# An adaLN decode step: the last 96 rows of the gate's modulation regrouped, from five pieces to four, and dealt over other transfers

## The chip, the cores and the metric

The kernel runs on one core of one Trainium2 chip. The metric is the device time of one execution in microseconds (us); less is better. Times are medians of several runs. One more execution was taken with the hardware profiler; all rows quoted as profile come from it. Engines: PE (TensorE), DVE (VectorE), ACT (ScalarE), POOL (GpSimd), SP (SyncE, which here only issues transfers), and 16 DMA engines that move the data.

## The reference

One decode step of a transformer block with modulation from a condition `c`, for a batch of 2 and one token each:

```
mod = silu(c) @ w_mod                 # 512 -> 6 * 512: sa, ca, ga, sb, cb, gb
h = layernorm(x) * (1 + ca) + sa
x = x + ga * attention(h)             # 32 heads of 128, 4096 cached positions each
h = layernorm(x) * (1 + cb) + sb
x = x + gb * (mish(h @ w1 + b1) @ w2) # 512 -> 1376 -> 512
```

`gb`, the last gate, is the sixth block of `mod`: `silu(c)` (512 values for each of the two) times `w_mod[:, 2560:3072]`, a matrix of 512 x 512. The change is about how a part of that matrix comes into the core. Nearly all bytes are the caches of keys and values.

## The kernel before

All inputs are laid out on the host as a sequence of loads. Each load fills a tile `room` of 128 partitions with up to 64 KB in each; three such tiles take turns, and a load is issued when the tile's earlier contents have been used. `load(n)` issues the transfers of load `n` on SP's queue: whole transfers of 128 rows at L153, and for a transfer with fewer rows (a "loose" one), four transfers that take every fourth row, at L156 (`STEP = 4`).

A head's keys are multiplied with the query on DVE (`products`, L336) and summed (`sums`, L339). The softmax's weights go to PE, where `weighted_v` (L379) multiplies them with the head's values. After the last head come, in this order on PE: the last head's values, the output projection (`head_out_q`), the norm, the modulation of the second half, the first dense layer (`w1ps`, L573), the transposes back (`fps`, L588), the hidden layer's activation on DVE and ACT (L602 to L609), and the second dense layer (`yps`, L618), eleven groups of four products. `busy(n)` (L316) issues products of `n` blocks of 128 columns whose result nobody reads, two blocks a product; they keep PE going between steps. A float32 product shows in the profile as two matmuls (x2).

The gate's matrix has 512 rows. They are multiplied in `modulation_5` (L538), one term after another into one sum in PSUM:

- `M5 = 3` blocks of 128 rows, which come with the last load;
- `REST` = 32 rows that lie in an otherwise empty part of the second layer's first chunk;
- the other 96 rows, in "pieces". Each piece is a row group on the first partitions of a tile, 512 columns (2 KB) a row. `PIECES = (20, 20, 20, 20, 16)`: the first four stand side by side in one array `m5p` of 20 rows of 8 KB, the fifth in an array `m5q` of 16 rows of 2 KB.

The last two loads look like this (a part is a list of contents and the widths of its transfers, in float32 numbers a row):

```
[([("m5q", 0)], (512,)), ([("m4", 0)] + last[6:], (W + HALF, W, W)), ([("m5p", 0)], (512 * WHOLE,))],
[
    ([("m3", 0), ("w1", 0)], (W + 2 * sum(WIDTHS), 2 * sum(WIDTHS))),
    ([("m5", 0), ("w2", 0)], (512 * (M5 + 1), 5 * 512, 3 * 512, 512, 512)),
],
```

So the last load but one has four transfers of 4 rows of 2 KB (`m5q`), three transfers with the fifth modulation block and the last head's values (3072, 1024 and 1024 KB), and four transfers of 5 rows of 8 KB (`m5p`). The last load has seven transfers of 128 rows, 2400 KB down to 256 KB. On PE, terms 0 and 1 are multiplied before the norm, 2 and 3 during it, term 4 (`m5q`) between `h2ps` and `w1ps`, and the rest after `fps`.

Of the kernel before, what the change touches and what calls it, by code (L numbers as in the profile page):

```python
# [8 lines left out]
F32 = mybir.dt.float32  # L9
# [4 lines left out]
P = 128  # L14
WIDTHS = (384, 384, 352, 256)
CHUNKS = [(g, j) for j in range(3) for g in range(4) if WIDTHS[g] > P * j]
STEP = 4
PIECES = (20, 20, 20, 20, 16)
WHOLE = PIECES.count(PIECES[0])
M5 = 3  # L20
REST0 = WIDTHS[2] - 2 * P
REST = 512 - P * M5 - sum(PIECES)
# [3 lines left out]
W = 2048  # L26
HALF = BIG // 2
SIZES = {
    "k": BIG, "v": HALF, "wq": W, "wo": W, "m01": 2 * W, "m2": W, "m3": W, "m4": W, "m5": 512 * M5,
    "m5p": 512 * WHOLE, "m5q": 512, "w1": 4 * sum(WIDTHS), "w2": 512 * len(CHUNKS),  # L30
}
OUT_STEP = 1
AHEAD = (14, 22)
# [3 lines left out]
def stream():  # L37


    order, n_v = [], 0  # L40
    for h in range(1, HEADS):
        order.append(("k", h))
        if h % HC == HC - 1 and HC < h < HEADS - 1:
            c = (h + 1) // HC
            order.append([("wq", c), ("wo", c - 2)])
        if h not in AHEAD:
            order += [("v", n_v, 0), ("v", n_v, 1)]
            n_v += 1
    order = [x if isinstance(x, list) else [x] for x in order]

    def size(x):
        return sum(SIZES[key[0]] for key in x)

    loads = [[([("m01", 0), ("wq", 0), ("wq", 1)], (4 * W,)), ([("k", 0)], (BIG,))]]
    for _ in range(1, HEADS):
        row = []
        while size(row) < ROW:
            room = ROW - size(row)
            row += order.pop(next(i for i, x in enumerate(order) if size(x) <= room))
        loads.append([(row, (ROW,))])  # L60
    last = [("v", h, i) for h in range(HEADS - 4, HEADS) for i in range(2)]
    assert order == [[key] for key in last[:2]], order
    loads += [
        [(last[:2] + [("wo", 6), ("wo", 7), ("m2", 0)], (BIG + 3 * W,))],
        [(last[2:4], (BIG,)), (last[4:6], (BIG,))],
        [([("m5q", 0)], (512,)), ([("m4", 0)] + last[6:], (W + HALF, W, W)), ([("m5p", 0)], (512 * WHOLE,))],
        [
            ([("m3", 0), ("w1", 0)], (W + 2 * sum(WIDTHS), 2 * sum(WIDTHS))),
            ([("m5", 0), ("w2", 0)], (512 * (M5 + 1), 5 * 512, 3 * 512, 512, 512)),
        ],  # L70
    ]
    return loads
# [3 lines left out]
def kernel(  # L76
# [17 lines left out]
    nc = tc.nc  # L94
# [4 lines left out]
    G = D // P  # L99
# [8 lines left out]
    NCH = len(CHUNKS)  # L108
    NP5 = len(PIECES) + 1

    const = ctx.enter_context(tc.tile_pool(name="const", bufs=1))
# [13 lines left out]
    def take(t, keys):  # L125
        lo = 0
        for key in keys:
            kind, n = key[:2]
            part = t[:, lo : lo + SIZES[kind]]
            lo += SIZES[kind]  # L130
            if kind == "k":
                k_t[n] = part.rearrange("p (j d) -> p j d", d=DH)
            elif kind == "v":
                v_t[n, key[2]] = part.rearrange("p (c n) -> p c n", n=512)
            elif kind in ("wq", "wo"):
                (wq_t if kind == "wq" else wo_t)[n] = part.rearrange("p (k n) -> p k n", k=G)
            else:
                w_t[kind] = part.rearrange("p (k n) -> p k n", k={"w2": NCH, "m5": M5, "m5p": WHOLE, "m5q": 1}.get(kind, G))

    w_t = {}  # L140
    done = set()

    def load(n):

        t = kvp.tile([P, ROW], F32, tag="room", name=f"room{n}", bufs=3)
        lo = 0
        for keys, srcs in loads[n]:
            take(t[:, lo:], keys)
            for src in srcs:
                rows, width = src.shape  # L150
                dst = t[:rows, lo : lo + width]
                if rows == P:
                    nc.sync.dma_start(out=dst, in_=src)  # L153
                else:
                    for i in range(STEP):
                        nc.sync.dma_start(out=dst[i::STEP], in_=src[i::STEP])  # L156
                lo += width

    loaded = 0

    def used(*keys):
# [26 lines left out]
        out=fold, in_=ident.rearrange("p (g r) -> p r g", g=G), axis=AX.X, op=ALU.add  # L188
# [3 lines left out]
        out=mean_w, in0=fold[:, None, :].to_broadcast([P, G, R]), scalar1=1.0 / D, scalar2=None, op0=ALU.mult  # L192
# [4 lines left out]
        out=half, in_=ident.rearrange("p (b r) -> p r b", b=B), axis=AX.X, op=ALU.add  # L197
# [5 lines left out]
    for b in range(B):  # L203
        nc.vector.memset(same[PB * b : PB * (b + 1), b, :], 1.0)
    same = same.rearrange("p b r -> p (b r)")
    eps_t = const.tile([P, 48], F32, name="eps_t")
    nc.vector.memset(eps_t, EPS)

    ct = const.tile([P, G, R], F32, name="ct")
# [2 lines left out]
    ct5 = const.tile([P, NP5, R], F32, name="ct5")  # L212
# [99 lines left out]
    def busy(n, bank=1):  # L312

        for lo in range(0, n, 2):
            cols = P * min(2, n - lo)
            nc.tensor.matmul(ov[bank][:, :cols], lhsT=ident, rhs=e_t[0].rearrange("p c m -> p (c m)")[:, :cols], start=True, stop=True)  # L316
# [131 lines left out]
    for h in range(H):  # L448
# [38 lines left out]
        out=ct5[:, :, ::TB],  # L487
# [38 lines left out]
    w1_t, w2_t = w_t["w1"], w_t["w2"]  # L526
    gps = ov[1 - N % 2][:, :P]
    rest5 = slice(REST0, REST0 + REST)
    wm5p = [w_t["m5p"][:, n, :] for n in range(WHOLE)] + [w_t["m5q"][:, 0, :]]
    terms5 = [(ct5[:rows, n, :], wm5p[n][:rows]) for n, rows in enumerate(PIECES)]  # L530
    terms5 += [(ct[:, k, :], wm5[:, k, :]) for k in range(M5)]
    terms5.append((ct5[rest5, len(PIECES), :], w2_t[rest5, 0, :]))

    def modulation_5(lo, hi):
        for n in range(lo, hi):
            c, w = terms5[n]
            for g in range(G):
                nc.tensor.matmul(  # L538
                    gps[R * g : R * (g + 1)], lhsT=c, rhs=w[:, P * g : P * (g + 1)],
                    start=(n == 0), stop=(n == len(terms5) - 1),  # L540
                )
# [20 lines left out]
    h2ps = columns(hq, "h2ps")  # L562
    nc.vector.tensor_copy(h2t[:, :, ::TB], h2ps)

    busy(1)
    modulation_5(4, len(PIECES))
    hq_pad = work.tile([P, 512], F32, tag="o", name="hq_pad")
    nc.gpsimd.memset(hq_pad[:, : NJ * P], 0.0)
    w1ps = wide_ps("w1ps")
    for k in range(G):  # L570
        lo = 0
# [9 lines left out]
    lo = 0  # L581
# [49 lines left out]
def _lay_out(np, a):  # L631


    def rows(w):

        return w.reshape(-1, P, w.shape[-1]).transpose(1, 0, 2)

    def q_rows(v):

        return v.reshape(2, 4, P).transpose(1, 0, 2).reshape(8, P)  # L640

    B, H, S, DH = a["A_k_cache"].shape
    kv = {
        kind: a[n].reshape(B, H, P // B, -1).transpose(1, 0, 2, 3).reshape(H, P, -1)
        for kind, n in (("k", "A_k_cache"), ("v", "A_v_cache"))
    }
    wq = rows(a["A_wq"]).reshape(P, 4, 8, 512).transpose(2, 0, 1, 3).reshape(8, P, -1)
    wo = a["A_wo"].reshape(8, 4, P, 512).transpose(0, 2, 1, 3).reshape(8, P, -1)
    wm = rows(a["w_mod"])
    w1 = rows(a["B_w1"])  # L650
    starts = np.cumsum((0,) + WIDTHS)
    b1c = np.zeros((P, 12 + 2 * (len(PIECES) + 1)), a["B_b1"].dtype)
    m5 = a["w_mod"][:, 512 * 5 :]
    m5p, f0 = np.zeros((P, len(PIECES) + 1, 512), m5.dtype), P * M5
    for n, size in enumerate(PIECES + (REST,)):
        to = REST0 if n == len(PIECES) else 0
        b1c[to : to + size, 12 + 2 * n : 14 + 2 * n] = a["c"].reshape(2, 512)[:, f0 : f0 + size].T
        m5p[to : to + size, n] = m5[f0 : f0 + size]
        f0 += size
    w2 = np.zeros((P, len(CHUNKS), 512), a["B_w2"].dtype)  # L660
    for n, (g, j) in enumerate(CHUNKS):
        f0 = starts[g] + P * j
        f1 = min(f0 + P, starts[g + 1])
        b1c[: f1 - f0, n] = a["B_b1"][f0:f1]
        w2[: f1 - f0, (n + 1) % len(CHUNKS)] = a["B_w2"][f0:f1]
    w2[REST0 : REST0 + REST, 0] = m5p[REST0 : REST0 + REST, -1]

    pieces = {**kv, "wq": wq, "wo": wo, "m01": [wm[:, :, :1024]], "w1": [w1], "w2": [w2], "m5p": [m5p[:, :WHOLE]], "m5q": [m5p[:, WHOLE]], "m5": [rows(m5)[:, :M5]]}
    for n in (2, 3, 4):
        pieces[f"m{n}"] = [wm[:, :, 512 * n : 512 * (n + 1)]]  # L670
    def piece(kind, n, part=None):
        row = pieces[kind][n].reshape(P, -1)
        return row if part is None else row[:, HALF * part : HALF * (part + 1)]

    loose = {"m5p": PIECES[0], "m5q": PIECES[-1]}
    arrays = {
        "head": np.stack([q_rows(a["c"]), q_rows(a["A_x"])], axis=1),
        "b1c": b1c,
    }
    for n, parts in enumerate(stream()):  # L680
        for i, (keys, widths) in enumerate(parts):
            row = np.concatenate([piece(*key) for key in keys], axis=1)
            cuts = np.split(row, np.cumsum(widths)[:-1], axis=1)
            for j, t in enumerate(cuts):
                arrays[f"load{n}_{i}_{j}"] = np.ascontiguousarray(t[: loose[keys[0][0]]] if keys[0][0] in loose else t)
    return arrays
# [28 lines left out]
```

## Time and profile before

| what | us |
|---|---|
| median of 3 runs (lowest to highest) | 695.18 (695.08 to 695.32) |
| profiled execution, whole time | 694.79 |
| its span, first to last instruction | 693.4 |
| DVE busy | 588.4 (85%) |
| PE busy, matmuls | 291.3 (42%) |
| last head's last values have landed | 672.9 from the span's start |
| the output's transfer is issued | 691.8 from the span's start |

The difference between span and whole time lies around the program's instructions. In rows of the chain, the numbers are the start and the length in us, then the engine, the tile written, and the line. In rows of the timeline stand start, length, engine, line, operation, tiles, shapes, count, and in brackets how long the engine was idle before and what ended that. `SPq` is SP's queue of instructions: an issue of a transfer.

### The profile page before, as it was taken

Reading aid. Unit: us, or ns where it says so; the run is one execution under the profiler, and the core shown is the slowest. Engines: PE = TensorE matmul, PEld = TensorE weight load, DVE = VectorE, ACT = ScalarE, POOL = GpSimd, SP = SyncE. Lnnn points to the kernel's source line nnn. Section 1 sums busy time; section 2 is a strip of 40 time slices with the busy share of each in tenths; the row PEclk is TensorE's granted clock in tenths of the full one; section 3 lists DMA queues with packets and bytes.
Section 4 is the critical chain, followed back from the end, with each engine's and each line's share of the span. In section 5 each row is a group of like instructions: output and inputs, shape, how many; then the busy total and the mean of one; then the engine's idle time right before and its main releaser. Section 6 shows DMA issues by size and latency. Waiting matters only on the chain.

```text
span 693.4 us, 4061 instructions
## 1 busy us (share of the span) xinstructions
PE 291.3 (42%) x1704; PEld 109.5 (16%) x1704; DVE 588.4 (85%) x223; ACT 44.2 (6%) x169; POOL 4.4 (1%) x20
## 2 busy tenths in 40 slices
PE   3403334335145624335232716235324426134898
PEld 1200001001012201101100301011101111001345
DVE  3799899999999999999999999999999999899102
ACT  1000000000000000000000000000000010000011
POOL 2000000000000000000000000000000000000000
PEclk9855666669565566556575565656585656656799
DMA  9999999999999999999999999999999999999997
GB/s 389 459 423 423 424 423 480 417 427 431 423 447 446 428 423 436 423 446 440 427 427 439 440 439 427 427 443 427 439 439 421 431 450 421 446 420 421 431 428 308
DMA packets 7019, 297.48 MB, mean 429 GB/s; under 512 B 941, under 2 KB 1077, under 8 KB 1477
## 3 DMA queue, kind: packets, MB, share of 16 engines
q1 hardware_dynamic: 6696, 297.14, 99.2%
q8 instruction: 13, 0.21, 0.1%
q10 hardware_dynamic: 304, 0.09, 0.1%
q14 instruction: 6, 0.04, 0.0%
HBM read 297.16 MB, written 0.07 MB: 429 GB/s over the span
## 4 chain that ended last, share of the span: by engine, by line
DMA 68%; DVE 28%; PE 4%; issue 0%; ACT 0%; SPq 0%; DVEq 0%; ACTq 0%
DMA room<-in_load 68%; DVE room L336 14%; DVE s L339 14%; PE modps L265 1%; PE ov L316 1%; PE qps L309 1%; PE yps L618 0%; PE w1ps L573 0%; PE ov L538 0%; PE ov L379 0%; PE fps L588 0%; PE otp L402 0%; DVE m L352 0%; DVE hcw L298 0%; ACT q L310 0%
## 5 line engine op out<-in xcount | busy, mean ns | idle before, releaser
L336 DVE TENSOR_TENSOR room<-room,q 128x8192 f32<-128x8192 f32 x32 | 278.2, 8692 | 45.5 <-DMA room<-in_load 41.1
L339 DVE TENSOR_REDUCE s<-room 128x64 f32<-128x8192 f32 x32 | 277.9, 8683 | 0.4 <-DVE m L352 0.3
L379 PE MATMUL ov<-room,e 128*32 128x512 f32 x1024 | 174.7, 836 | 73.0 <-ACT e L355 63.3
L348 PE MATMUL mt<-d,same 128*128 128x64 f32 x64 | 18.7, 388 | 195.7 <-DVE d L346 195.7
L379 PEld LDWEIGHTS ov<-room,e 128*32 128x32 f32 x1024 | 39.1, 145 | 178.0 <-issue 131.2
L355 ACT ACTIVATE e<-s,m 64x64 f32<-64x64 f32 x64 | 22.1, 345 | 554.3 <-DVE m L352 553.5
L348 PEld LDWEIGHTS mt<-d,same 128*128 128x128 f32 x64 | 13.5, 264 | 225.5 <-DVE d L346 180.3
L309 PE MATMUL qps<-room,hcw 128*128 128x512 f32 x64 | 42.5, 829 | 4.2 <-DMA room<-in_load 3.4
L363 PE MATMUL l<-l,ones 128*128 128x8 f32 x16 | 4.6, 358 | 74.9 <-ACT e L355 74.9
L402 PE MATMUL otp<-pick,o 128*128 128x8 f32 (+2 forms) x72 | 14.3, 326 | 34.0 <-ACT o L394 32.1
L309 PEld LDWEIGHTS qps<-room,hcw 128*128 128x128 f32 x64 | 16.5, 270 | 25.4 <-issue 20.0
L402 PEld LDWEIGHTS otp<-pick,o 128*128 128x128 f32 x72 | 13.6, 282 | 42.5 <-ACT o L394 39.8
L394 DVE COPY o<-ov 128x256 f32<-128x256 f32 x1 | 0.4, 425 | 22.9 <-ACT o L394 22.9
L363 PEld LDWEIGHTS l<-l,ones 128*128 128x128 f32 x16 | 3.8, 295 | 76.3 <-ACT e L355 76.3
L352 DVE TENSOR_REDUCE m<-mt 128x1 f32<-128x64 f32 x32 | 7.0, 217 | 6.6 <-PE mt L348 6.6
L410 PE MATMUL att<-room,ot 128*32 128x512 f32 x62 | 10.2, 719 | 5.2 <-DMA room<-in_load 4.6
L355 ACT ACTIVATION_READ_ACCUMULATOR e<-s,m 64x1 f32 x64 | 11.8, 185 | 0.0
L316 PE MATMUL ov<-e,ident 128*128 128x256 f32 (+1 forms) x44 | 11.0, 380 | 0.0
L346 DVE TENSOR_SCALAR d<-half,m 128x64 f32<-128x64 f32 x32 | 8.1, 254 | 1.1
L316 PEld LDWEIGHTS ov<-e,ident 128*128 128x128 f32 x44 | 7.6, 190 | 3.8 <-issue 3.1
L344 DVE TENSOR_REDUCE m<-s 128x1 f32<-128x64 f32 x32 | 6.9, 217 | 0.9
L265 PE MATMUL modps<-room,ct 128*32 128x128 f32 (+1 forms) x128 | 7.0, 363 | 1.2 <-DMA room<-in_load 1.2
(107 smaller groups left out, 69.5 us busy)
## 6 DMA issues: line engine op xcount, KB each, us to landing
room<-in_load SPq DMA_DIRECT2D x4, 4096.0 KB, 24.9
room<-in_load SPq DMA_DIRECT2D x1, 7168.0 KB, 39.2
room<-in_load SPq DMA_DIRECT2D x1, 3072.0 KB, 23.3
room<-in_load SPq DMA_DIRECT2D x3, 1024.0 KB, 22.0
room<-in_load SPq DMA_DIRECT2D x1, 2400.0 KB
room<-in_load SPq DMA_DIRECT2D x1, 1376.0 KB, 14.1
room<-in_load SPq DMA_DIRECT2D x1, 1280.0 KB, 14.6
room<-in_load SPq DMA_DIRECT2D x1, 768.0 KB
```

The costliest lines, as they stand in the source:

```text
L265: nc.tensor.matmul(ps[R * g : R * (g + 1)], lhsT=ct[:, k, :], rhs=t[:, k, :].rearrange("p (m n) -> p m n", m=n)[:, :, P * g : P * (g + 1)] ...
L309: nc.tensor.matmul(ps, lhsT=hcw[:, k, :], rhs=wq_t[ch][:, k, :], start=(k == 0), stop=(k == G - 1))
L316: nc.tensor.matmul(ov[bank][:, :cols], lhsT=ident, rhs=e_t[0].rearrange("p c m -> p (c m)")[:, :cols], start=True, stop=True)
L336: nc.vector.tensor_tensor(out=k_t[h], in0=k_t[h], in1=qv, op=ALU.mult)
L339: nc.vector.tensor_reduce(out=s_t[h], in_=k_t[h], axis=AX.X, op=ALU.add)
L346: nc.vector.tensor_scalar(out=d, in0=half, scalar1=m_t[h][:, 0:1], scalar2=None, op0=ALU.mult)
L348: nc.tensor.matmul(mps[h], lhsT=same, rhs=d, start=True, stop=True)
L355: nc.scalar.activation(e_t[i][own_b, :, M * i + 4 * b : M * i + 4 * b + 4], s_t[h][own_b].rearrange("p (c m) -> p c m", m=4), AF.Exp, bias ...
L363: nc.tensor.matmul(lps[n], lhsT=ones, rhs=sum_t[n % 2], start=True, stop=True)
L379: nc.tensor.matmul(ov[bank][R * g : R * (g + 1), :], lhsT=e_t[h % HC][:, NB // 2 * part + c, :], rhs=v_t[h, part][:, c, :], start=(first a ...
L402: nc.tensor.matmul(tps[:, x], lhsT=o_t[m], rhs=pick_t[n][:, m, x], start=(m == 0), stop=(m == 3),)
L410: nc.tensor.matmul(att[R * i : R * (i + 1), :], lhsT=ot_t[n % 2][:, i, :], rhs=wo_t[n][:, i, :], start=(n == 0), stop=(n == H // HC - (2 i ...
```

## The change

The 96 rows are cut into four pieces of 24 rows instead of four of 20 and one of 16. All four stand side by side, so there are 24 rows of 8 KB and no rows of 2 KB; `m5q` and its place in the layout are gone. The 24 rows are issued as eight transfers of 1, 1, 1, 3, 3, 5, 5 and 5 rows (`DEAL`), of which the first three (`EARLY`), with one row each, go ahead of the values and the other five behind them. On PE the fifth piece's products between `h2ps` and `w1ps` are gone, and `busy(1)` at that place is now `busy(3)`. A constant tile is made wider by 32 columns; the tile of the condition's pieces is 32 columns narrower.

```diff
-STEP = 4
-PIECES = (20, 20, 20, 20, 16)
-WHOLE = PIECES.count(PIECES[0])
+EARLY = 3
+DEAL = [slice(21, 22), slice(22, 23), slice(23, 24), slice(15, 21, 2), slice(16, 21, 2), slice(0, 15, 3), slice(1, 15, 3), slice(2, 15, 3)]
+PIECES = (24, 24, 24, 24)
+WHOLE = len(PIECES)
...
-        [([("m5q", 0)], (512,)), ([("m4", 0)] + last[6:], (W + HALF, W, W)), ([("m5p", 0)], (512 * WHOLE,))],
+        [([("m4", 0)] + last[6:], (W + HALF, W, W)), ([("m5p", 0)], (512 * WHOLE,))],
...
-        lo = 0
+        lo, parts, early = 0, [], []
         for keys, srcs in loads[n]:
             take(t[:, lo:], keys)
             for src in srcs:
                 rows, width = src.shape
                 dst = t[:rows, lo : lo + width]
+                lo += width
                 if rows == P:
-                    nc.sync.dma_start(out=dst, in_=src)
+                    parts.append((dst, src))
                 else:
-                    for i in range(STEP):
-                        nc.sync.dma_start(out=dst[i::STEP], in_=src[i::STEP])
-                lo += width
+                    deals = [(dst[deal], src[deal]) for deal in DEAL]
+                    early, parts = deals[:EARLY], parts + deals[EARLY:]
+        for dst, src in early + parts:
+            nc.sync.dma_start(out=dst, in_=src)
...
-    eps_t = const.tile([P, 48], F32, name="eps_t")
+    eps_t = const.tile([P, 80], F32, name="eps_t")
...
-    wm5p = [w_t["m5p"][:, n, :] for n in range(WHOLE)] + [w_t["m5q"][:, 0, :]]
-    terms5 = [(ct5[:rows, n, :], wm5p[n][:rows]) for n, rows in enumerate(PIECES)]
+    terms5 = [(ct5[:rows, n, :], w_t["m5p"][:rows, n, :]) for n, rows in enumerate(PIECES)]
...
-    busy(1)
-    modulation_5(4, len(PIECES))
+    busy(3)
...
```

More of the change, by code (lines that the diff above doesn't have):

```diff
@@ L29 @@
     "k": BIG, "v": HALF, "wq": W, "wo": W, "m01": 2 * W, "m2": W, "m3": W, "m4": W, "m5": 512 * M5,
-    "m5p": 512 * WHOLE, "m5q": 512, "w1": 4 * sum(WIDTHS), "w2": 512 * len(CHUNKS),
+    "m5p": 512 * WHOLE, "w1": 4 * sum(WIDTHS), "w2": 512 * len(CHUNKS),
 }
@@ L137, in take @@
             else:
-                w_t[kind] = part.rearrange("p (k n) -> p k n", k={"w2": NCH, "m5": M5, "m5p": WHOLE, "m5q": 1}.get(kind, G))
+                w_t[kind] = part.rearrange("p (k n) -> p k n", k={"w2": NCH, "m5": M5, "m5p": WHOLE}.get(kind, G))
     w_t = {}
@@ L666, in _lay_out @@
     w2[REST0 : REST0 + REST, 0] = m5p[REST0 : REST0 + REST, -1]
-    pieces = {**kv, "wq": wq, "wo": wo, "m01": [wm[:, :, :1024]], "w1": [w1], "w2": [w2], "m5p": [m5p[:, :WHOLE]], "m5q": [m5p[:, WHOLE]], "m5": [rows(m5)[:, :M5]]}
+    pieces = {**kv, "wq": wq, "wo": wo, "m01": [wm[:, :, :1024]], "w1": [w1], "w2": [w2], "m5p": [m5p[:, :WHOLE]], "m5": [rows(m5)[:, :M5]]}
     for n in (2, 3, 4):
@@ L673, in piece @@
         return row if part is None else row[:, HALF * part : HALF * (part + 1)]
-    loose = {"m5p": PIECES[0], "m5q": PIECES[-1]}
+    loose = {"m5p": PIECES[0]}
     arrays = {
```

## The prediction

> **What bounds the kernel now.** I read the page first (parts 1 to 4), then the chain that ended last near its end, then the transfers' issues on SP's queue, then busy shares by stretch for the last microseconds.
>
> ```profile
> span 693.4 us, 4061 instructions
> q1 hardware_dynamic: 6696, 297.14, 99.2%
> HBM read 297.16 MB, written 0.07 MB: 429 GB/s over the span
> DMA 68%; DVE 28%; PE 4%; issue 0%; ACT 0%; SPq 0%; DVEq 0%; ACTq 0%
> ```
>
> SP's queue q1 keeps the 16 DMA engines busy for 99.2% of the span. The DVE share of the chain is only the work that frees a buffer for the next load. So time falls if fewer bytes are moved, or if the end is shorter: from the last values' landing on, the chain is on PE.
>
> The chain of work that ended last, its end:
>
> ```profile
> 672.88 0.04 issue
> 672.92 1.07 PE ov L379 x8
> 673.99 0.85 PE ov L316 x4
> ...
> 678.25 0.78 PE ov L316 x4
> ...
> 681.41 0.32 PE h2ps L255 x2
> 681.73 0.32 PE ov L316 x2
> 682.05 0.35 PE ov L538 x8
> 682.40 2.76 PE w1ps L573 x16
> ...
> 687.65 0.63 PE ov L316 x2
> 688.27 2.32 PE yps L618 x80
> 690.60 0.03 issue
> 690.63 0.47 PE yps L618 x8
> ```
>
> Two things end almost together. PE has worked without a pause worth naming since 672.92 (the last quarter of the last head's values), and reaches the last group of the second dense layer (L618, the final x8) at 690.60. That group needs the last load, and PE's weight loads show how long it was missing:
>
> ```profile
> 688.20 2.12 PEld L618 LDWEIGHTS yps<-room,actt 96*32 96x32 f32 x80 [0.33 <-issue]
> 690.63 0.16 PEld L618 LDWEIGHTS yps<-room,actt 128*32 128x32 f32 x8 [0.30 <-DMA room<-in_load]
> 681.77 0.17 DVE L563 COPY h2t<-h2ps 128x8 f32<-128x8 f32 x1 [0.85 <-PE h2ps L255]
> 677.30 0.64 PE L538 MATMUL ov<-room,ct 20*32 20x128 f32 x16
> ```
>
> The weight load waited 0.30 us for the DMA, but the chain as a whole lost 0.03. An earlier last landing alone is therefore worth 0.03 us on the chain; a later one costs its full lateness; a longer PE chain costs its full length.
>
> **The change, part by part.**
>
> *Bytes.* Before: 20 rows of 8 KB and 16 of 2 KB, 192 KB. After: 24 of 8 KB, 192 KB. At 429 GB/s that is 0.46 us before and after: 0. The bias transfer loses two columns in its rows; it goes at the very start on ACT's queue beside the first loads: 0.
>
> *Transfers.* Four small ones, three of values, four small before (11); three, three, five after (11). On SP's queue, by time of issue:
>
> ```profile
> 641.80 2.66 SPq L156 DMA_DIRECT2D room<-in_load  x4
> 644.51 0.44 SPq L153 DMA_DIRECT2D room<-in_load  x1
> 650.90 0.33 SPq L153 DMA_DIRECT2D room<-in_load  x1
> 660.56 2.88 SPq L156 DMA_DIRECT2D room<-in_load  x4
> 665.28 0.34 SPq L153 DMA_DIRECT2D room<-in_load  x1
> 667.82 0.33 SPq L153 DMA_DIRECT2D room<-in_load  x1
> 672.89 0.33 SPq L153 DMA_DIRECT2D room<-in_load  x1
> ```
>
> The issues at 644.51 and 650.90 by size, and the output's, with the time to landing:
>
> ```profile
> room<-in_load SPq DMA_DIRECT2D x1, 3072.0 KB, 23.3
> room<-in_load SPq DMA_DIRECT2D x1, 1024.0 KB, 22.0
> out<-y ACTq DMA_DIRECT2D x1, 64.0 KB, 1.6
> ```
>
> A small transfer costs SP about 0.7 us (2.66 and 2.88 for four). With one less ahead of the values these are issued some 0.7 us sooner; they wait behind older loads anyhow, since the 3072 KB one lands 23.3 us after its issue: 0. The rows also show a rule of the queue: a transfer is issued when the one eight places before it has landed. The second transfer of the last load went out at 667.82, and 644.51 + 23.3 = 667.81 is the landing of the 3072 KB one, eight before it; 650.90 + 22.0 = 672.9 released the fourth (672.89). Moving the small ones shifts this count by one: the *first* transfer of the last load is now the eighth after the 3072 KB one, so it leaves at about 667.82 and not at 665.28, 2.54 us later. The ones behind it leave at 670.25 and 672.89, one place later each. What hides it: the engines still have the 1024 KB of values and the rows, which land by 672.88. Whether the first engines to finish run dry: the busy shares below put engines up to 3 us apart, so the earliest may finish at about 669.9, 2.1 us after the new issue. The one transfer on an idle queue, the output, took 1.6 us from issue to landing as a whole. So 0; if it does not hold, the dry time falls on the engines that are earliest, with up to 3 us to spare.
>
> *The pieces' wait.* Their first use on PE is at 677.30. Rows behind the values: five transfers, at most five rows on one engine. A row of 8 KB at a sixteenth of 429 GB/s takes 0.305 us (an estimate), so 672.88 + 1.5 = 674.4 at worst: 2.9 us of cover. The first matmul now waits for all the small transfers at once instead of half of them; they have landed alike: 0. Uncovered, each us would go on PE's chain.
>
> *PE at L538 and L316.* Removed: the fifth piece, 0.35 us (x8), with the filler of one block ahead of it, 0.32 (x2): 0.67 us between the transposed h2 and the first dense layer. Added: a filler of three blocks, a 256-column and a 128-column product. The same filler stands twice on the chain, 0.85 and 0.78 (x4); by its parts it would be 0.63 + 0.32 = 0.95. So +0.11 to +0.28. It is not hidden: h2t is done at 681.77 + 0.17 = 681.94 and the dense layer starts only at 682.40, when PE is through its queue. A gain is excluded, since every row of the longer filler is above 0.67. I take 0.85, the nearer row in the middle: +0.18. Everything behind (the copies, the hidden layer, yps) moves with it. The final x8 then starts at 690.60 + 0.18 = 690.78 instead of 690.63: +0.15. The rows in a piece (24 instead of 20) change no column count: 0.
>
> *Which engine carries the rows.* Busy shares by stretch at the end (after the core's stretch and its length come the engines' busy times, then clock, DMA share, GB/s):
>
> ```profile
> 686.00:687.00 1.00, 1.00 (x25) 0.98 (x28) 0.18 (x1) 0.22 (x1) 0.00 (x0) 1.00 0.98 406
> 687.00:688.00 1.00, 1.00 (x22) 0.47 (x14) 0.89 (x6) 0.00 (x0) 0.00 (x0) 1.00 0.82 328
> 688.00:689.00 1.00, 1.00 (x31) 0.80 (x33) 0.25 (x2) 0.00 (x0) 0.00 (x0) 1.00 0.59 231
> 689.00:690.00 1.00, 1.00 (x48) 1.00 (x43) 0.00 (x0) 0.00 (x0) 0.00 (x0) 1.00 0.40 145
> 690.00:691.00 1.00, 0.97 (x32) 0.48 (x20) 0.00 (x0) 0.00 (x0) 0.00 (x0) 1.00 0.02 6
> ```
>
> The engines do not end together: from 687 on they drop out, and in 689 to 690 some six of sixteen (0.40) still move data. So it matters on which engine a row lies. The trace does not number engines, so I bound it. If each transfer starts at the same engine and gives one row to each, the first engine had four rows of 8 KB and four of 2 KB (4 x 0.305 + 4 x 0.076 = 1.53 us) and now has eight of 8 KB (2.44): +0.91; the second and third have 5 x 0.305 = 1.53: 0; the fourth and fifth, three rows, 0.92: -0.61 and -0.30. If rows were spread over all engines: 0. Lower end for the last landing: the late engine is the fourth, -0.61 or until the next late one ends; on the chain that is worth 0.03 at most, and nothing once PE is longer. Upper end: it is the first, +0.91. I take 0, as the middle of the two and because eleven engines hold no row and the late ones are six. Ahead of the values the first engine has 3 x 0.305 = 0.92 us instead of 0.31; that delays PE's start at 672.92 only if this engine is the last one there too, by up to 0.61.
>
> [...] No row of this trace shows an engine's number. [...]
>
> Sum: bytes 0, queue 0, wait 0, PE +0.15, rows 0: +0.15 us. The profiled execution took 694.79 us (span 693.4 and 1.4 around it), so 694.94; the median of the timed runs, 695.18, lies 0.39 above, so 695.33, say 695.3.
>
> **The rivals.**
>
> *The first engine becomes the last (slower).* Place: the last transfers of the last load. For: eight rows in one column where the others have five or three; engines end 3 us apart; six of sixteen are late. Against: the late ones need not include this one. Price: up to +0.91 on a landing that is now tied with PE, so 690.6 goes to 691.5 and the time to 696.1. It decides when that engine ends later than PE's new 690.78, that is, when before it ended after 690.6 - 0.91 + 0.18, about 689.9; below that it costs nothing.
>
> *The edit does nothing.* For: the longer filler replaces work of like length, the next product may overlap its tail, bytes and transfer count are equal, and the last landing may come earlier. Against: the chain shows 0.78 and 0.85 where 0.67 goes. Then the 0.03 of waiting is all there is: 695.15.
>
> *The late issue opens a gap.* For: 2.54 us later. Against: 1.6 us from issue to landing on an idle queue beside 2.1 us of cover. Price: the missing time on all engines if the cover is gone, about 1 us: 696.2. It decides only if transfers behind loaded engines need above 2.1 us to start.
>
> **How the numbers follow.** Forecast 0.58, does nothing 0.19, first engine 0.18, gap 0.05. The range takes the low end below "does nothing" by the scatter of the runs and something for the unknown, 694.7, and the high end at the two slower rivals, 696.2. A bound of 0.2%, about what a measurement of this kernel can tell from no change, is 1.39 us: 693.8 and 696.6. All cases lie inside it. Slower needs the first engine's 0.91 together with the 0.61 at the front: 0.04. Faster needs 1.4 us that no row offers: 0.02. Same: 0.94.
>
> **What would show it.** Right: the chain's stretch from h2ps to w1ps grows from 0.67 to 0.8 or 0.9 us; SP issues the last load's first transfer near 667.8; the last values land at 672.9 as before; the final x8 has no DMA wait. Wrong: that x8 waits for DMA and starts beyond 691 (first engine); DMA share dips between 669 and 671 (gap); L573 starts within 0.75 us of the filler (nothing). It fails as a whole if the values' landing moves by over 1 us, which no bound above allows.

## The result, and the profile after

The changed kernel takes 696.16 us (median of 22 runs), against 695.19 for the kernel before in the same session: ratio 1.0016, 95% interval 1.0010 to 1.0022, some 1.0 us slower. The forecast was 695.3, between 694.7 and 696.2, and no change. The time lies at the upper end of the range, and the move, though small, is clear of the noise, which the forecast denied. The profiled execution took 695.64 us (span 694.2).

The end of the chain, after (start, length, what):

```profile
675.18 16.26 DMA room<-in_load
691.44 0.04 issue
691.49 0.47 PE yps L619 x8
691.96 0.02 issue
691.98 0.30 DVE y L626
```

Before, the chain ran through PE's work from 672.9 to 690.6, but for 0.5 us around a copy on ACT (from 685.2 to 685.7). Now the chain's last stretch is one wait of 16.26 us for the last transfer of the last load, and the final x8 starts at 691.49 instead of 690.63: +0.86 us, which is the whole difference of the two profiled executions (695.64 - 694.79 = 0.85).

The timeline of PE and PEld, after:

```profile
673.41 1.07 PE L382 MATMUL ov<-room,e 128*32 128x512 f32 x8 [1.39 <-DMA room<-in_load]
682.08 0.90 PE L319 MATMUL ov<-e,ident 128*128 128x256 f32 x4
682.91 2.77 PE L574 MATMUL w1ps<-room,h2t 128*32 128x384 f32 x32
691.48 0.16 PEld L619 LDWEIGHTS yps<-room,actt 128*32 128x32 f32 x8 [0.43 <-DMA room<-in_load]
```

The last values, too, landed later: PE took them up at 673.41 and not at 672.92 (+0.49). The longer filler starts at 682.08 and the dense layer at 682.91 (before: 682.40), so PE is late by about as much as the values.

Where do the transfers lose the time? The stretch from 670 to 674, in which the last values, the rows of the pieces and the first transfer of the last load are moved, before and then after (the last two columns are the DMA share and GB/s; both count a packet, the trace's record of a piece of a transfer, where it starts, with its whole time and size, so a share can pass 1):

```profile
670.00:674.00 4.00, 3.03 (x50) 1.10 (x41) 0.00 (x0) 0.00 (x0) 0.00 (x0) 1.00 1.06 445
```

```profile
669.00:670.00 1.00, 0.98 (x16) 0.26 (x8) 0.00 (x0) 0.00 (x0) 0.00 (x0) 1.00 1.09 443
670.00:671.00 1.00, 0.70 (x8) 0.29 (x12) 0.00 (x0) 0.00 (x0) 0.00 (x0) 1.00 1.11 394
671.00:672.00 1.00, 1.00 (x28) 0.57 (x20) 0.00 (x0) 0.00 (x0) 0.00 (x0) 1.00 1.14 351
672.00:673.00 1.00, 0.02 (x3) 0.00 (x0) 0.00 (x0) 0.00 (x0) 0.00 (x0) 1.00 1.02 318
670.00:674.00 4.00, 2.31 (x40) 1.01 (x40) 0.00 (x0) 0.00 (x0) 0.00 (x0) 1.00 1.05 364
```

This is the telling pair of columns. The DMA share is as before (1.06, 1.05), so by this measure the engines were as busy as before; but they moved 364 GB/s instead of 445. The packets took longer. Over 4 us the 81 GB/s are 324 KB, and at 429 GB/s that is 0.76 us: nearly all of the 0.86.

The times of the single packets, which the two traces hold, say which ones. Of those that start between 667 and 676, all 201 packets of 8 KB took 0.309 us before, and 114 of the 115 packets of 19,200 bytes about 0.714. After, 41 of 207 and 35 of 97 took over 5% longer, up to 0.77 and 1.47 us. The pieces' rows are at most 24 of these packets, and the packets of 19,200 bytes are rows of the last load's first transfer, which writes all 128 partitions in both kernels. So packets that the change does not touch became slow too. The times above 0.309 and 0.714 add up to 12.7 us, or 0.79 us for each of 16 engines (0.03 before).

### The profile page after: what moved, and what is told of

The parts are those of the page before. It is cut to its first block, busy times and chain, and to the rows that moved or that the text cites. A ratio compares the mean times of both kernels' runs of the same rounds, so it can differ in the third digit from the quotient of the medians.

```text
span 694.2 us, 4049 instructions
## 1 busy us (share of the span) xinstructions
PE 289.1 (42%) x1698; PEld 108.5 (16%) x1698; DVE 586.4 (84%) x223; ACT 44.2 (6%) x169; POOL 4.5 (1%) x20
## 3 DMA queue, kind: packets, MB, share of 16 engines
q1 hardware_dynamic: 6672, 297.14, 99.2%
## 4 chain that ended last, share of the span: by engine, by line
DMA 67%; DVE 30%; PE 1%; SPq 0%; issue 0%; ACT 0%; DVEq 0%
DMA room<-in_load 67%; DVE room L339 15%; DVE s L342 15%; PE qps L312 1%; PE modps L268 1%; SPq L160 0%; DVE m L355 0%; DVE hcw L301 0%; PE hps L258 0%; ACT q L313 0%; PE yps L619 0%; DVE y L626 0%; DVE hq L292 0%; DVE hq L291 0%; DVE y L627 0%
## 5 line engine op out<-in xcount | busy, mean ns | idle before, releaser
L382 PE MATMUL ov<-room,e 128*32 128x512 f32 x1024 | 170.3, 819 | 70.3 <-ACT e L358 50.0
L312 PE MATMUL qps<-room,hcw 128*128 128x512 f32 x64 | 45.0, 872 | 4.5 <-DMA room<-in_load 3.7
```

The source lines that it names most:

```text
L312: nc.tensor.matmul(ps, lhsT=hcw[:, k, :], rhs=wq_t[ch][:, k, :], start=(k == 0), stop=(k == G - 1))
L382: nc.tensor.matmul(ov[bank][R * g : R * (g + 1), :], lhsT=e_t[h % HC][:, NB // 2 * part + c, :], rhs=v_t[h, part][:, c, :], start=(first a ...
```

## The experiments

Three theories stood after this profile. *Partitions*: what slows the packets is which partitions the rows are written to. *First engine*: eight rows on the first engine make it late (the slower rival of the prediction, which had given 696.1, as it happens the measured time). *Late issue*: the last load's first transfer leaves 2.5 us later.

A word on what "misplaced" means below. Take a transfer's rows in their order and the partitions in groups of four (0 to 3, 4 to 7, and so on): a row is in place if it is the transfer's first and lies in the first group, its second and lies in the second group, and so on; otherwise it is called misplaced. The kernel before takes every fourth row (0, 4, 8, 12, 16), so none is misplaced. The changed kernel takes 21, 22, 23 alone; 15, 17, 19; 16, 18, 20; and every third row of the first 15: 18 of 24 are. The expectation of the first run puts the theory by the engines that write the partitions, and rows are counted on engines in several places below. Both assume that a transfer's rows lie, in their order, on engines one, two, three and so on. No row of a trace numbers engines, so this was not shown; what the runs show is the time by partition. That a row which goes alone is not split fits the count of packets: those of 8,192 bytes rise from 415 to 419 with the change, as the rows of 8 KB do from 20 to 24, and those on SP's queue fall from 6696 to 6672, by two for each of the 12 rows that are no longer there.

Times are medians; ratios are of the means, against the kernel before in the same session, with 95% intervals.

### Neighbouring rows in the kernel before

```diff
-                        nc.sync.dma_start(out=dst[i::STEP], in_=src[i::STEP])
+                        deal = slice(5 * i, 5 * i + 5) if rows == PIECES[0] else slice(i, rows, STEP)
+                        nc.sync.dma_start(out=dst[deal], in_=src[deal])
```

> The kernel before, with one difference: each of the four transfers of five 8 KB rows takes five neighbouring rows (0 to 4, 5 to 9, ...) instead of every fourth. Order, sizes and count of transfers, rows per engine and PE's work are those of before. Theory 'partitions' (a row is slow, and slows others, when the DMA engine that writes it is not the one that writes these partitions in the 128-row transfers; four neighbouring partitions go together; 16 of the 20 rows are then misplaced, 18 of 24 in the changed kernel): slower by 0.4 to 1.2 us, 695.6 to 696.4, and GB/s between 670 and 674 falls below 400 as in the changed kernel. Theory 'first engine' (the rows moved to the first engine make it the last): 695.2, no change. Theory 'late issue' (the last load's first transfer leaves 2.5 us later): 695.2, no change.

Measured: 696.75, ratio 1.0029 (1.0017 to 1.0041), slower still than the changed kernel, and above the range that "partitions" gave (695.6 to 696.4). The same stretch of its trace:

```profile
670.00:674.00 4.00, 2.16 (x36) 1.01 (x40) 0.00 (x0) 0.00 (x0) 0.00 (x0) 1.00 1.07 346
```

Nothing but the rows' dealing differs from the kernel before, and the slow stretch is there: 346 GB/s at a share of 1.07.

### The changed kernel with its rows in place

```diff
-DEAL = [slice(21, 22), slice(22, 23), slice(23, 24), slice(15, 21, 2), slice(16, 21, 2), slice(0, 15, 3), slice(1, 15, 3), slice(2, 15, 3)]
+DEAL = [slice(20, 21), slice(21, 22), slice(22, 23), slice(3, 15, 4), slice(15, 24, 4), slice(0, 20, 4), slice(1, 20, 4), slice(2, 20, 4)]
```

> The changed kernel, with one difference: which of the 24 partitions each transfer takes. Still 1, 1, 1, 3, 3, 5, 5, 5 rows in the same order, with the same rows per engine, but by steps of four, so that 6 of 24 rows are misplaced in the sense of the theory 'partitions' and not 18. 'Partitions': the slow stretch at 670 to 674 goes (GB/s back above 410), 695.2 to 695.7. 'First engine' and 'late issue': 696.1, as the changed kernel.

Measured: 695.17, ratio 1.0001 (0.9992 to 1.0010): the time of the kernel before, 0.03 us under the range that "partitions" gave. By the assumption the first engine still carries eight rows; the transfers have as many rows each as in the changed kernel and still leave in the same order.

```profile
670.00:674.00 4.00, 3.17 (x52) 1.16 (x44) 0.00 (x0) 0.00 (x0) 0.00 (x0) 1.00 1.01 418
```

The loss is undone by the choice of partitions alone. "First engine" falls. The chain ends on PE again and shows the filler in its place:

```profile
681.48 0.32 PE h2ps L258 x2
681.80 0.76 PE ov L319 x4
682.55 2.76 PE w1ps L574 x16
```

### Six rows a transfer

```diff
-EARLY = 3
-DEAL = [slice(21, 22), ...]
+EARLY = 0
+DEAL = [slice(i, 24, 4) for i in range(4)]
```

> The changed kernel with its 24 rows as four transfers of six rows, every fourth row, all behind the values: no row misplaced, four rows on each of six engines, nothing ahead of the values, and the last load's first transfer not held back. 'Partitions': 695.1 to 695.4 (the longer filler alone is left, 0.1 us). 'First engine': also 695.1 to 695.4. 'Late issue': also. If it stays at 696, all three fall, and PE's filler or the 24-row pieces are the cause.

Measured: 695.54 (694.64 to 696.30), ratio 1.0003 (0.9994 to 1.0012). It lies 0.1 us above what all three theories gave (695.1 to 695.4), within the scatter, so it does not choose between them; it rules out the 24-row pieces and the filler as the cause of a whole microsecond.

### Late issue alone

One transfer of the 2 KB rows goes behind the values (`later`), the rest is the kernel before.

```diff
+                        if rows == PIECES[-1] and i == STEP - 1:
+                            later.append((dst[i::STEP], src[i::STEP]))
```

> The kernel before, with one of the four transfers of 2 KB rows moved behind the values, so that three small transfers stand ahead and five behind as in the changed kernel, and the last load's first transfer is the eighth after the 3072 KB one and leaves near 667.8 instead of 665.3. Rows, partitions and engines as before. 'Late issue': slower by 0.5 to 1 us, 695.7 to 696.2. 'Partitions' and 'first engine': 695.2, no change.

Measured: 695.18, ratio 0.9999 (0.9990 to 1.0007). Its queue of issues:

```profile
667.96 0.34 SPq L153 DMA_DIRECT2D room<-in_load  x1
672.76 0.33 SPq L153 DMA_DIRECT2D room<-in_load  x1
```

The last load's first transfer left at 667.96, as meant, and the third at 672.76, and it cost nothing. "Late issue" falls.

### Source or destination

Neighbouring rows are neighbours in memory and in the partitions. Two kernels part the two by permuting the rows in memory on the host.

```diff
# destination misplaced, source as before
+                        here = slice(5 * i, 5 * i + 5) if rows == PIECES[0] else slice(i, rows, STEP)
+                        nc.sync.dma_start(out=dst[here], in_=src[i::STEP])
# destination as before, source neighbouring
+                        there = slice(5 * i, 5 * i + 5) if rows == PIECES[0] else slice(i, rows, STEP)
+                        nc.sync.dma_start(out=dst[i::STEP], in_=src[there])
```

> The kernel with five neighbouring rows a transfer, but with the rows in memory permuted so that the source is read in the order of the kernel before (every fourth row); only the destination partitions are misplaced. 'Partitions': as with neighbouring rows on both sides, 696.3 to 697.0. Rival 'source' (the reads from memory collide when a transfer's rows are neighbours there): 695.2, as before.

> The mirror of it: the kernel before with its destination (every fourth partition), while each transfer reads five neighbouring rows of memory. 'Partitions': 695.2, as before. 'Source': 696.3 to 697.0.

Measured: destination misplaced 697.42, ratio 1.0043 (1.0026 to 1.0059); source alone 695.18, ratio 0.9999 (0.9991 to 1.0008). The first is again above its range (696.3 to 697.0), and above the 696.75 of neighbouring rows on both sides, though these two intervals overlap. The stretch, first with the destination and then with the source changed:

```profile
670.00:674.00 4.00, 2.06 (x44) 0.93 (x36) 0.00 (x0) 0.00 (x0) 0.00 (x0) 1.00 1.06 325
```

```profile
670.00:674.00 4.00, 2.98 (x52) 1.03 (x43) 0.00 (x0) 0.00 (x0) 0.00 (x0) 1.00 1.03 434
```

The write side decides (697.42, 325 GB/s); the order of the reads does not matter here (695.18, 434 GB/s).

### One group too far, in place, and half of each

All three have transfers of 1, 1, 1 rows ahead of the values and 1, 5, 5, 5, 5 behind, by the assumption eight rows on the first engine and four on each of the next four. Only the partitions differ.

```diff
# one group too far: 20 of 24 misplaced
+DEAL = [slice(i, i + 1) for i in range(4)] + [slice(i, 24, 4) for i in range(4, 8)]
# in place: 4 of 24
+DEAL = [slice(i, i + 1) for i in range(20, 24)] + [slice(i, 20, 4) for i in range(4)]
# half: 12 of 24
+DEAL = [slice(0, 1), slice(1, 2), slice(22, 23), slice(23, 24), slice(2, 20, 4), slice(3, 20, 4), slice(4, 21, 4), slice(5, 22, 4)]
```

> The changed kernel's order and rows per engine almost kept (1, 1, 1 ahead; 1, 5, 5, 5, 5 behind), every fourth row, but the five-row transfers start one group of four partitions too far: 20 of 24 rows misplaced, each transfer's rows in five different groups, by one group each. It tells two forms of 'partitions' apart. If any row in another engine's group is slow: 696 or more, GB/s at 670 to 674 below 400. If only several rows of one transfer in the same group are slow (crowding, as with 0 to 4): 695.0 to 695.5.

> The same transfers in the same order with the same rows per engine as the kernel whose five-row transfers start one group too far, but these now start in their own group (0 to 3) and the four single rows lie in group five: 4 of 24 rows misplaced instead of 20. 'Partitions': 695.0 to 695.6 where the other gave 697.7. If the shape of the transfers (four of five rows, singles) is what costs: 697 or more.

> Again the same transfers, order and rows per engine; two of the four five-row transfers start in their own group and two one group too far: 12 of 24 rows misplaced (10 of 20 in the five-row ones). 'Partitions' with a price for each row: about half the delay of the last landing between 4 and 20 misplaced rows, which was 692.72 with 20 and about 690.6 with the rows in place, so 691.5 to 691.9, and 696.0 to 696.6 in time. If one late engine alone counts and not the number of rows: as with 20 or as with 4.

Measured: one group too far 697.68, ratio 1.0041 (1.0029 to 1.0053); in place 694.97, ratio 1.0001 (0.9992 to 1.0010), 0.03 us under its range; half 695.90, ratio 1.0025 (1.0005 to 1.0045). The stretch in the same order:

```profile
670.00:674.00 4.00, 2.07 (x42) 0.98 (x35) 0.00 (x0) 0.00 (x0) 0.00 (x0) 1.00 1.08 293
```

```profile
670.00:674.00 4.00, 2.97 (x45) 1.19 (x42) 0.00 (x0) 0.00 (x0) 0.00 (x0) 1.00 1.02 429
```

```profile
670.00:674.00 4.00, 2.16 (x44) 1.01 (x40) 0.00 (x0) 0.00 (x0) 0.00 (x0) 1.00 1.04 345
```

With one and the same shape, order and count, 4, 12 and 20 misplaced rows give 429, 345 and 293 GB/s. Several rows in one group are not needed; each transfer of the first kernel has its rows in five groups. The final x8's weight load, with half misplaced and with the rows in place:

```profile
691.52 0.16 PEld L619 LDWEIGHTS yps<-room,actt 128*32 128x32 f32 x8 [0.31 <-DMA room<-in_load]
```

```profile
690.63 0.16 PEld L619 LDWEIGHTS yps<-room,actt 128*32 128x32 f32 x8 [0.31 <-DMA room<-in_load]
```

With half the last landing is at 691.48, at the lower edge of the range that a price for each row gave (691.5 to 691.9); the time, 695.90, fell just below its range (696.0 to 696.6). Two of its 12 times are 700.24 and 703.62 and lift the mean, so the ratio says more than the medians, which differ by 0.80 us. With 20 the last landing is at 692.72, but the time does not end on it: the chain ends on PE, which the last section takes up.

### The shorter filler

```diff
-    busy(3)
+    busy(1)
     hq_pad = work.tile([P, 512], F32, tag="o", name="hq_pad")
```

Applied to the changed kernel with its rows in place.

> The version with 6 misplaced rows, and with the filler of one block instead of three between the transposed h2 and the first dense layer. In its trace the chain ends on PE and the filler takes 0.76 us there, so with 0.32 the end comes 0.3 to 0.4 us sooner, until the last landing binds: 694.8 to 695.0, below both kernels. If the landing binds at once: 695.2.

Measured: 695.33, ratio 1.0002 (0.9993 to 1.0010): no gain shows, though a gain of 0.3 us would lie within this interval. The trace settles it. Its end:

```profile
674.87 15.73 DMA room<-in_load
690.61 0.04 issue
690.65 0.47 PE yps L619 x8
```

With a shorter PE chain the last landing binds at once, at 690.61, where it was in the kernel before. No version tried here beats that kernel.

## Why the prediction was wrong

*Bytes, count of transfers, SP's queue: right, with one slip.* The queue's rule of eight places held: after, the last values landed at 673.37, and the transfer eight places on left at 673.38. The slip: the forecast had the values issued 0.7 us sooner, but a single row cost SP 0.29, 0.23 and 0.24 us, so the first of the three left 1.7 us sooner (642.80), and by the rule of eight the last one 7.2 us sooner (643.68 and not 650.90). Late issue alone has that one at 644.84 and costs nothing. The forecast was an issue near 667.8 for the first transfer of the last load, with no dry engine; the issue, and the one that waits for the last values, after:

```profile
667.86 0.35 SPq L160 DMA_DIRECT2D room<-in_load  x1
673.38 0.33 SPq L160 DMA_DIRECT2D room<-in_load  x1
```

The DMA share shows no dip between 669 and 671 (1.09, 1.11), and late issue alone costs nothing. The gap rival was rightly set low.

*PE's filler: right in kind, too large in size.* Forecast 0.85 us against 0.67, so +0.18. Where PE carries the chain it took 0.76, so +0.09. In the changed kernel it is hidden, since the last landing ends later than PE's chain.

*Which engine carries the rows: this step failed.* The term "rows 0" measured +0.86 us on the last landing. The step priced a row by its length on the engine that carries it, 0.305 us, and asked only whether that engine is late; with that, "the fourth engine -0.61, the first +0.91" were the bounds and 0 the value taken. That each transfer starts at the same engine and gives one row to each was its assumption; no run shows it, nor on which engine a row lies. A packet of 8 KB did take 0.309 us in the kernel before, where every row is in place; but the step left out that the time depends on the partitions that the rows write, and for packets of other transfers too: after, 41 of 207 packets of 8 KB and 35 of 97 of the last load's first transfer took over 5% longer. The sign "the last values land at 672.9 as before" failed with it: PE took them up 0.49 us later. And no transfer needs to have more rows for that: with the same number of rows in each transfer, in the same order, and 6 rows misplaced instead of 18 the time is 695.17.

*The slower rival came to the right time by a wrong mechanism.* It gave 696.1 for an overloaded first engine, and 696.16 was measured; the run with the rows in place has, by the rival's own count, the same eight rows there and took 695.17, so the agreement is chance.

What the runs show of the partitions is this. Only the destination matters (697.42 with it misplaced, 695.18 with the source changed alone). All four places within a group are as good: the four transfers of the kernel before start at 0, 1, 2 and 3, and all 201 packets of 8 KB between 667 and 676 took 0.309 us. A shift by one group is enough to lose (697.68). And the number of groups that a transfer reaches is not the measure: the shifted five-row transfers reach five groups, as those in place do, and yet the stretch has 293 GB/s and not 429.

What stays open is the size, and how one misplaced row slows others. The packet times above 0.309 and 0.714 us, counted as in the section on the result, come for each of 16 engines to 0.03 us before, 0.11 with 4 misplaced rows, 0.15 with 6, 0.91 with 12, 0.79 with 18 (the changed kernel) and 1.64 with 20: they grow with the count, but the count alone does not give them. With 16 of 20 misplaced, the same partitions gave 1.04 with neighbouring rows on both sides and 1.27 with the destination alone. With 20 misplaced rows, 51 of 76 packets of 19,200 bytes between 667 and 676 were over 5% longer than 0.714 us. These are rows of a 128-row transfer, so the loss reaches beyond the rows that the deal moves; by what path, no run here shows.

## What to carry to other kernels

When a transfer has few rows, choose the partitions that it writes as carefully as the number of rows: every fourth row, so that the first lies in the first group of four, the second in the second and so on, and not neighbouring ones. Here the kernels with at most 6 misplaced rows had 418 to 447 GB/s between 670 and 674, and those with 12 or more 293 to 364. A DMA share as high as before with fewer GB/s (1.05 and 364 against 1.06 and 445) meant here that packets took longer, and no sum over bytes shows it. And where two chains end within 0.1 us of each other, as here, a gain on one is worth next to nothing (the shorter filler), while a loss on either can count in full (a last landing 0.86 us later, and 0.85 us more for the profiled execution).

## What the hardware showed that was not expected

In the kernel moved one group too far, the last values came so late that PE stood still for 2.26 us before them, and the granted clock, 1.00 from 658 on, was halved about a microsecond after it had resumed. The timeline's row, and the stretches behind it (the clock is the third column from the end):

```profile
674.33 1.06 PE L382 MATMUL ov<-room,e 128*32 128x512 f32 x8 [2.26 <-DMA room<-in_load]
```

```profile
674.00:675.00 1.00, 0.68 (x8) 0.16 (x8) 0.00 (x0) 0.00 (x0) 0.00 (x0) 1.00 1.01 384
675.00:676.00 1.00, 1.00 (x6) 0.59 (x3) 0.08 (x1) 0.37 (x1) 0.00 (x0) 0.63 0.81 346
676.00:678.00 2.00, 2.00 (x11) 1.91 (x9) 0.34 (x1) 0.00 (x0) 0.26 (x1) 0.50 1.03 443
682.00:684.00 2.00, 1.95 (x28) 1.50 (x24) 0.80 (x4) 0.02 (x1) 0.00 (x0) 0.98 1.00 425
```

The same filler that takes 0.85 us on the chain elsewhere took 1.58 there:

```profile
674.33 1.06 PE ov L382 x8
675.39 1.58 PE ov L319 x4
```

So that execution lost twice: late data, and then a PE at half its clock until about 682. After waits of 1.39 us (the changed kernel) and 1.80 (destination misplaced) no such fall is in the profiled executions: the clock there is 1.00 from 674 to 686. This one took 699.26 us, where its kernel's five times have a median of 697.68. Times above 699 us came in 9 of the 53 timed executions of kernels with 12 or more misplaced rows, and in none of the 66 of the others tried; whether the clock fell in each of the nine, no trace shows. The fall followed a wait of 2.26 us in one execution; what sets it off, no run here shows.
